# Windowed attention in front of two feed-forward layers: cells of 32 queries by 64 keys, four heads to a unit

## The chip, the cores and the metric

The kernel runs on one core of one Trainium2 chip. The time is device microseconds from launch to end, the median of three runs. TensorE (PE in the profile) multiplies, VectorE (DVE) and ScalarE (ACT) do the elementwise work, SyncE (SP) issues every DMA on one queue. [...]

## The reference

Batch 4, 8 heads, 576 positions, head size 64; 2304 tokens in all, model width 512, hidden width 2048. Everything is fp32.

```python
scores = scale * np.matmul(q, k.transpose(0, 1, 3, 2))
rel = pos[:, None] - pos[None, :]
mask_plain = (rel >= 0) & (rel < 32)                       # heads 0 to 3
mask_dil = (rel >= 0) & (rel < 128) & (rel % 4 == 0)       # heads 4 to 7
attn = softmax of scores where the mask holds, else -1e9
x = np.matmul(attn, v)                                     # (2304, 512)
h = x @ w_in                                               # first layer
g = (a0 + a1*h + a2*h2 + a3*h3) / (1 + |b0|*|h| + |b1|*h2 + 1e-6)
x = g @ w_out
h = x @ w_in2                                              # second layer
out = (max(h, 0) + alpha * min(h, 0)) @ w_out2
```

A query attends to 32 keys at most: the last 32 positions, or, for the dilated heads, 32 positions at a distance of 4. Taken by their remainder modulo 4, the positions of a dilated head form four streams, and in a stream the window is again the last 32.

## The kernel before, in words

The 2304 tokens are six blocks of 384. Attention works in 24 units, U = 0 to 23, four to a block: two plain, then two dilated. Before the change a unit is two heads and two segments of 192 tokens. A plain unit cuts a segment in three tiles of 64 queries by 96 keys, a dilated one in four tiles of 48 by 80. For each unit the code has these steps.

- `att_s` (L444 to L488): the mask is written into PSUM banks aS and aP by bf16 matmuls with an identity (L461), and the scores are added by fp32 matmuls (L481) in 64x64 quarters of the array, four at a time. The profile shows each fp32 matmul of this kind as two MATMUL instructions.
- `att_max` (L495, L499, VectorE), `att_exp` (L515, ScalarE, one instruction for each tile, with a sum), `att_den` (L525, L526), and the normalisation: `att_norm` (L535, ScalarE) or, for units 0 to 3, `att_norm2` (L544, VectorE).
- `att_t` (L552): TensorE transposes each tile into aS and aP. `att_tev` (L571, ScalarE; L573, VectorE, for one of two in units 0 to 3) copies the two banks into the SBUF tile pts.
- `att_pv` (L585): probabilities times values, 128 rows by 64 columns of the array, two at a time, into a bank of the ring ps_h, which has two banks and which the first layer uses too. `att_hi` (L612, ScalarE) copies the result to xh, `att_lo` (L618, VectorE) the rest to xl, since the large matmuls take a value as a high and a low part.

Units 0 to 4 come first. Then a loop over J = 0 to 47 takes two chunks of 128 hidden columns of the first layer at each J: `inproj` (L648) into ps_h, `rat_1` and `rat_2` (L666 to L680) for the rational function, `g_split` (L687, L688), `outproj` of J-2 (L698) into four banks ps_y. For block 0 (J = 0 to 7) the weights are unsplit fp32 (16 MATMUL instructions a J and layer half), later they are split (24 instructions). One unit U = 4 + (J+1)//2 is worked in every two J: at odd J `att_pv(U-1)`, `att_s(U)`, `att_hi(U-1)`, `att_lo(U-1)`, `att_max`, `att_exp`, `att_den`, half of `att_norm`; at even J the other half, `att_t` and `att_tev`. Attention ends with unit 23, before J = 40. `w_convert` (L378 to L399) turns float64 weights into fp32 words on ScalarE and VectorE; `w_early` does so for 13 weight pairs of the second layer from J = 16 on. The second layer (L717, L839 and L745 to L874) has no attention.

A planner, `in_order_of_need`, sets the order of instructions on each engine for the first 197 us from estimated costs (`_cost`); after that program order holds. SyncE's DMAs keep program order; at the start that is the string `ORDER`, in which q and v are the two loads of a unit, w a weight chunk, c the masks, i the fp32 identity, p coefficients.

Of the kernel before, what the change touches and what calls it, by code (L numbers as in the profile page):

```python
# [34 lines left out]
FILL = 256  # L35
ORDERED = 197e3
# [3 lines left out]
ORDER = "cqiqpvqvqvvwwwwwwqvwwwwwwwwqv"  # L40


class Shape:


    def __init__(self, dilated):
        self.dil = dilated
        self.nt = DIL if dilated else 3
        self.nq = SEG // self.nt
        self.nk = self.nq + WIN  # L50
        self.m = 2 * self.nq
        self.rows = 64 + self.nq
        self.step = self.nk if dilated else self.nq
        self.kw = self.nt * self.nk if dilated else SEG + WIN
        self.qk = SEG + self.kw
        self.vw = self.nt * 128
# [46 lines left out]
def _cost(i):  # L103
# [6 lines left out]
    if e == mybir.EngineType.PE:  # L110
        if ins[0].dtype == F32 and not i.is_transpose:
            if n > 128:
                return 645, 845
            return (40, 250) if i.tile_size[0] == 64 else (65, 270)
        if i.is_transpose:
            return 100, 300
        if ins[0].dtype == BF16:
            return (30, 230) if n < 256 else (0.42 * n, 0.42 * n + 200)
        return 0.45 * n, 0.45 * n + 200
# [150 lines left out]
def attn_rational_prelu_kernel(  # L270
    ctx: ExitStack,
    tc: tile.TileContext,
    qk_p: bass.AP,
    v_p: bass.AP,
    qk_d: bass.AP,
    v_d: bass.AP,
# [7 lines left out]
    eye: bass.AP,  # L284
# [26 lines left out]
    ident = cp.tile([128, 128], F32, name="ident")  # L311
    msk = cp.tile([128, consts.shape[1]], BF16, name="msk")
    ident16 = msk[:, 0:128]
    mask = {}
    o = 128
    for dil in (0, 1):
        for first in (0, 1):
            mask[dil, first] = msk[:, o:o + SHAPES[dil].nk]
            o += SHAPES[dil].nk
# [109 lines left out]
    def u_info(U):  # L429
        n, pair = divmod(U, 4)  # L430
        return n, pair, SHAPES[pair // 2]

    def u_load(U, what):
        n, pair, sh = u_info(U)
        i = n * 2 + pair % 2
        if U < 4:
            tag = f"{'in' if what == 'qk' else 'out'}l{8 + 2 * U}"
            t = wp.tile([128, 2 * DM], F32, tag=tag, name="ld_" + what)
        else:
            t = ldp.tile([128, 2 * DM], F32, tag=what, name="ld_" + what)  # L440
        if what == "qk":
            nc.sync.dma_start(out=t[:, :2 * sh.qk], in_=(qk_d if sh.dil else qk_p)[i])
        else:
            nc.sync.dma_start(out=t[:, :2 * sh.vw], in_=(v_d if sh.dil else v_p)[i])  # L444
        att.setdefault(U, {})[what] = t

    QUADS = ((0, 0), (1, 1), (0, 1), (1, 0))

    def att_s(U, tags=("aS", "aP")):

        blk, _, sh = u_info(U)
        a = att[U]
        ld = a["qk"]
        s = a["s"] = [bank(tag) for tag in tags]
        T, n, nq = sh.nt, sh.nk, sh.nq
        base = mask[sh.dil, 0]
        size = (64, nq)

        def put(h, g, t0, t1, mk):
            r = slice(64 * h, 64 * h + 64)  # L460
            nc.tensor.matmul(  # L461
                out=s[h][64 * g:64 * g + size[g], t0 * n:t1 * n].rearrange("p (t k) -> p t k", t=t1 - t0),
                lhsT=ident16[r, 64 * h:64 * h + size[g]],
                rhs=mk[r].unsqueeze(1).to_broadcast([64, t1 - t0, n]),
                start=(t0 == 0), stop=False,
            )

        for h, g in QUADS:
            if (2 * blk + g) % 3:
                put(h, g, 0, T, base)  # L470
            elif sh.dil:
                put(h, g, 0, T, mask[1, 1])
            else:
                put(h, g, 0, 1, mask[0, 1])
                put(h, g, 1, T, base)
        for t in range(T):
            for h, g in QUADS:
                r = slice(64 * h, 64 * h + 64)
                q0 = g * sh.qk + t * nq
                k0 = g * sh.qk + SEG + t * sh.step  # L480
                nc.tensor.matmul(  # L481
                    out=s[h][64 * g:64 * g + size[g], t * n:(t + 1) * n],
                    lhsT=ld[r, q0:q0 + size[g]],
                    rhs=ld[r, k0:k0 + n],
                    start=False, stop=(t == T - 1),
                )

    def att_max(U):  # L488
        _, _, sh = u_info(U)
        a = att[U]  # L490
        T, n, m = sh.nt, sh.nk, sh.rows
        mx = sp.tile([128, 8], F32, tag="mx", name="mx", bufs=2)
        nm = a["nm"] = sp.tile([128, 8], F32, tag="nm", name="nm", bufs=2)
        for h in range(2):
            nc.vector.tensor_reduce(  # L495
                out=mx[:m, h * T:(h + 1) * T], in_=a["s"][h][:m, :T * n].rearrange("p (t k) -> p t k", t=T),
                axis=AX.X, op=ALU.max, negate=True,
            )
        nc.vector.tensor_scalar_mul(out=nm[:m, :2 * T], in0=mx[:m, :2 * T], scalar1=scale)  # L499

    def att_exp(U):
        _, _, sh = u_info(U)
        a = att[U]
        T, n, m = sh.nt, sh.nk, sh.rows
        if U < 4:
            t = tp.tile([128, 2 * BLK], F32, tag="t" + "abca"[U], name="p", bufs=2)
            a["p"] = [t[:, :T * n], t[:, T * n:]]
            a["pp"] = t[:m, :2 * T * n].rearrange("p (t k) -> p t k", k=n)
        else:
            a["p"] = [ap_.tile([128, BLK], F32, tag="p", name="p") for _ in range(2)]  # L510
        sm = a["sm"] = sp.tile([128, 8], F32, tag="sm", name="sm", bufs=2)
        for h in range(2):
            for t in range(T):
                k = h * T + t
                nc.scalar.activation(  # L515
                    out=a["p"][h][:m, t * n:(t + 1) * n], in_=a["s"][h][:m, t * n:(t + 1) * n], func=AF.Exp,
                    scale=scale, bias=a["nm"][:m, k:k + 1], accum_out=sm[:m, k:k + 1],
                )

    def att_den(U):  # L520
        _, _, sh = u_info(U)
        a = att[U]
        w, m = 2 * sh.nt, sh.rows
        rd = a["rd"] = sp.tile([128, 8], F32, tag="rd", name="rd", bufs=2)
        nc.vector.tensor_scalar_add(out=a["sm"][:m, :w], in0=a["sm"][:m, :w], scalar1=1e-9)  # L525
        nc.vector.reciprocal(out=rd[:m, :w], in_=a["sm"][:m, :w])  # L526

    def att_norm(U, h):
        _, _, sh = u_info(U)
        a = att[U]  # L530
        T, n, m = sh.nt, sh.nk, sh.rows
        p, rd = a["p"][h], a["rd"][:, h * T:(h + 1) * T]
        for t in range(T):
            pv = p[:m, t * n:(t + 1) * n]
            nc.scalar.activation(out=pv, in_=pv, func=AF.Copy, scale=rd[:m, t:t + 1])  # L535

    def att_norm2(U):
        _, _, sh = u_info(U)
        a = att[U]
        T, n, m = sh.nt, sh.nk, sh.rows  # L540
        for h in range(2):
            pp = a["pp"][:, h * T:(h + 1) * T]
            rd = a["rd"][:m, h * T:(h + 1) * T].unsqueeze(2).to_broadcast([m, T, n])
            nc.vector.tensor_tensor(out=pp, in0=pp, in1=rd, op=ALU.mult)  # L544

    def att_t(U, h, tag):
        _, _, sh = u_info(U)
        a = att[U]
        T, n, r = sh.nt, sh.nk, sh.rows
        pt = bank(tag)  # L550
        for t in range(T):
# [657 lines left out]
```

## Time and profile before

| | |
|---|---|
| median of three runs | 886.04 us (884.64 to 886.32) |
| profiled execution: span from first to last instruction | 881.9 us |
| PE busy | 870.7 us, 99% |
| DVE busy | 760.0 us, 86% |
| ACT busy | 612.6 us, 69% |
| DMA | 92.78 MB, mean 105 GB/s |

The profiled execution's own time is known as its span; the median of the runs is 4.1 us above that span, for what lies around the first and the last instruction. Busy is the time in which at least one instruction of an engine runs. Matmuls overlap, so the time of one is read from the distance of starts and not from its duration.

### The profile page before, as it was taken

Reading aid. Unit: us, or ns where it says so; the run is one execution under the profiler, and the core shown is the slowest. Engines: PE = TensorE matmul, PEld = TensorE weight load, DVE = VectorE, ACT = ScalarE, POOL = GpSimd, SP = SyncE. Lnnn points to the kernel's source line nnn. Section 1 sums busy time; section 2 is a strip of 40 time slices with the busy share of each in tenths; the row PEclk is TensorE's granted clock in tenths of the full one; section 3 lists DMA queues with packets and bytes.
Section 4 is the critical chain, followed back from the end, with each engine's and each line's share of the span. In section 5 each row is a group of like instructions: output and inputs, shape, how many; then the busy total and the mean of one; then the engine's idle time right before and its main releaser. Section 6 shows DMA issues by size and latency. Waiting matters only on the chain.

```text
span 881.9 us, 14820 instructions
## 1 busy us (share of the span) xinstructions
PE 870.7 (99%) x5744; PEld 778.5 (88%) x5744; DVE 760.0 (86%) x1199; ACT 612.6 (69%) x1253; POOL 0.2 (0%) x4
## 2 busy tenths in 40 slices
PE   8999999999999999999999999999999999999998
PEld 6555679999999999999999999998889989899896
DVE  5999999989899998999999999998986778767652
ACT  6999988787877888887677576557564456645423
POOL 0000000000000000000000000000000000000000
PEclk9999999999999999999999999999999999999999
DMA  9964103124334534443021232323320011210001
GB/s 346 406 259 160 43 25 103 38 91 155 116 123 149 177 119 140 151 132 108 20 78 42 97 130 96 120 84 117 99 85 24 29 44 60 96 48 25 0 1 72
DMA packets 32902, 92.78 MB, mean 105 GB/s; under 512 B 3904, under 2 KB 11328, under 8 KB 32832
## 3 DMA queue, kind: packets, MB, share of 16 engines
q1 hardware_dynamic: 32832, 91.83, 30.1%
q8 instruction: 45, 0.74, 0.4%
q14 instruction: 25, 0.20, 0.1%
HBM read 76.61 MB, written 15.20 MB: 104 GB/s over the span
## 4 chain that ended last, share of the span: by engine, by line
PE 66%; ACT 15%; DVE 14%; DMA 3%; issue 2%; SPq 1%; ACTq 0%; DVEq 0%
PE ps_h L839 19%; PE ps_y L717 14%; PE ps_y L698 12%; PE ps_h L648 11%; PE ps_aS L717 4%; PE ps_aP L717 4%; ACT p L515 3%; ACT p L535 2%; DVE tc L679 2%; DVE tb L678 2%; DVE tc L680 2%; ACT tc L667 2%; ACT ta L676 2%; ACT ta L677 2%; DVE gl L688 1%
## 5 line engine op out<-in xcount | busy, mean ns | idle before, releaser
L648 PE MATMUL ps_h<-xh,winh 128*128 128x384 f32 x320 | 110.2, 344 | 1.9 <-DVE tc L669 1.7
L698 PE MATMUL ps_y<-gh,wouth 128*128 128x384 f32 x320 | 107.9, 339 | 0.0
L698 PE MATMUL ps_y<-gl,wouth 128*128 128x384 f32 x320 | 107.2, 335 | 0.2 <-DVE gl L688 0.2
L698 PE MATMUL ps_y<-gh,woutl 128*128 128x384 f32 x320 | 107.2, 335 | 0.0
L648 PE MATMUL ps_h<-xh,winl 128*128 128x384 f32 x320 | 107.1, 335 | 0.0
L648 PE MATMUL ps_h<-xl,winh 128*128 128x384 f32 x320 | 107.1, 335 | 0.0
L717 PE MATMUL ps_y<-wouth,gl 128*128 128x512 f32 x192 | 74.9, 390 | 0.0
L717 PE MATMUL ps_y<-woutl,gh 128*128 128x512 f32 x192 | 74.9, 390 | 0.0
L717 PE MATMUL ps_y<-wouth,gh 128*128 128x512 f32 x192 | 74.8, 390 | 0.0
L666 ACT ACTIVATE ta<-ps_h,root 128x384 f32<-128x384 f32 x96 | 56.7, 591 | 24.1 <-PE ps_h L648 23.9
L667 ACT ACTIVATE tc<-ps_h,co 128x384 f32<-128x384 f32 x96 | 66.0, 688 | 0.0
L648 PEld LDWEIGHTS ps_h<-xh,winh 128*128 128x128 f32 x320 | 60.0, 188 | 5.9 <-DVE tc L669 3.4
L745 ACT ACTIVATE gh<-tc 128x768 fp32r<-128x768 f32 x48 | 40.4, 841 | 30.5 <-PE ps_aP L717 28.0
L698 PEld LDWEIGHTS ps_y<-gl,wouth 128*128 128x128 f32 x320 | 60.1, 188 | 0.6 <-DVE gl L688 0.5
L648 PEld LDWEIGHTS ps_h<-xl,winh 128*128 128x128 f32 x320 | 60.1, 188 | 0.3
L745 ACT ACTIVATE st_a<-w 128x1024 fp32r<-128x1024 f32 x24 | 25.5, 1061 | 50.1 <-PE ps_h L839 41.5
L746 DVE TENSOR_TENSOR gl<-tc,gh 128x768 fp32r<-128x768 f32 x48 | 45.8, 955 | 16.8 <-ACT gh L745 16.7
L698 PEld LDWEIGHTS ps_y<-gh,wouth 128*128 128x128 f32 x320 | 60.1, 188 | 0.1
L648 PEld LDWEIGHTS ps_h<-xh,winl 128*128 128x128 f32 x320 | 60.1, 188 | 0.0
L698 PEld LDWEIGHTS ps_y<-gh,woutl 128*128 128x128 f32 x320 | 60.0, 188 | 0.0
L678 DVE SCALAR_TENSOR_TENSOR tb<-tb,ta 128x768 f32<-128x768 f32 x48 | 45.7, 953 | 15.4 <-ACT ta L677 15.1
L669 DVE SCALAR_TENSOR_TENSOR tc<-tc,co,ps_h 128x384 f32<-128x384 f32 x96 | 58.3, 608 | 0.5
(197 smaller groups left out, 2313.1 us busy)
## 6 DMA issues: line engine op xcount, KB each, us to landing
w<-w_dram_in SPq DMA_DIRECT2D x24, 512.0 KB, 3.6
raw<-in_w_in_dram SPq DMA_DIRECT2D x16, 512.0 KB, 4.7
raw_inh<-in_w_out_dram SPq DMA_DIRECT2D x13, 512.0 KB, 3.6
ld_qk<-in_qk_d_dram SPq DMA_DIRECT2D x12, 512.0 KB, 5.5
ld_v<-in_v_d_dram SPq DMA_DIRECT2D x12, 512.0 KB, 4.5
ld_qk<-in_qk_p_dram SPq DMA_DIRECT2D x12, 416.0 KB, 4.1
ld_v<-in_v_p_dram SPq DMA_DIRECT2D x12, 384.0 KB, 3.3
y_dram<-os SPq DMA_DIRECT2D x24, 192.0 KB, 1.9
```

Of the source, the lines that this page charges most:

```text
L515: nc.scalar.activation(out=a["p"][h][:m, t * n:(t + 1) * n], in_=a["s"][h][:m, t * n:(t + 1) * n], func=AF.Exp, scale=scale, bias=a["nm"][ ...
L535: nc.scalar.activation(out=pv, in_=pv, func=AF.Copy, scale=rd[:m, t:t + 1])
L648: nc.tensor.matmul(out=hp[:, :BLK], lhsT=w, rhs=x, start=(k == 0), stop=(k == len(pairs) - 1))
L666: nc.scalar.activation(out=ta, in_=hp, func=AF.Abs, scale=root)
L667: nc.scalar.activation(out=tc_, in_=hp, func=AF.Identity, scale=co[:, 3:4], bias=co[:, 2:3])
L669: nc.vector.scalar_tensor_tensor(out=tc_, in0=tc_, scalar=co[:, 1:2], in1=hp, op0=ALU.add, op1=ALU.mult)
L678: nc.vector.scalar_tensor_tensor(out=tb, in0=tb, scalar=C1, in1=ta, op0=ALU.add, op1=ALU.mult)
L698: nc.tensor.matmul(out=yt[:, :BLK], lhsT=w[:, m * 128:(m + 1) * 128], rhs=g, start=(c == 0 and i == 0), stop=(c == NC - 1 and i == len(pai ...
L717: nc.tensor.matmul(out=yt, lhsT=g[:, tok], rhs=w, start=(first and i == 0), stop=(last and i == 2))
L745: nc.scalar.activation(out=hi, in_=t, func=AF.Copy)
L746: nc.vector.tensor_tensor(out=lo, in0=t, in1=hi.bitcast(F32), op=ALU.subtract)
L839: nc.tensor.matmul(out=hp, lhsT=u[:, ws], rhs=x[:, xs], start=(k == 0), stop=(k == 5))
```

## The change

A unit is now four heads (the plain ones or the dilated ones) and 192 queries of each, in six cells of 32 queries by 64 keys; a plain unit is half a block of tokens, a dilated one two of the four streams of a block. Scores are 24 matmuls in 64x32 tiles of the array (eight tiles), the cells alternating between the upper and the lower 64 rows. The mask of a cell is one of four kinds, and neighbouring cells of one kind share a mask matmul. The probabilities of all cells lie in one tile of 128 partitions (32 for each head) by 384 columns. VectorE transposes its 32x32 blocks in one instruction, in place of TensorE's transposes and of their copies out of PSUM. Probabilities times values are matmuls of 32 rows by 64 columns, one for each head and block of 32 keys (28 in a plain unit, 32 in a dilated one), and go into aS and aP instead of ps_h, so `att_hi` and `att_lo` are two instructions of 192 columns each. `att_pv`, `att_hi` and `att_lo` of unit U are moved from the odd J that follows to the even J itself, after `inproj`; `att_s(U)` comes first in the odd J. The fp32 identity and its DMA are gone, queries and values of a unit share a load, and `ORDER` and the planner's costs differ.

```diff
-ORDER = "cqiqpvqvqvvwwwwwwqvwwwwwwwwqv"
+ORDER = "capaaawwwwwwawwwwwwwwa"
...
+        for jj in range(HALF):
+            for i in range(HEADS):
+                for p in range(2):
+                    at = jj * HEADS + i
+                    nc.tensor.matmul(
+                        out=s[p][quad(i), jj * CELL:(jj + 1) * CELL],
+                        lhsT=a["q"][rows(p), at * QB:(at + 1) * QB],
+                        rhs=a["k"][rows(p), at * CELL:(at + 1) * CELL],
+                        start=False, stop=(jj == HALF - 1),
+                    )
...
+        for p in range(2):
+            nc.vector.tensor_reduce(
+                out=mx[:, p * HALF:(p + 1) * HALF], in_=a["s"][p][:, :HALF * CELL].rearrange("p (t k) -> p t k", k=CELL),
+                axis=AX.X, op=ALU.max, negate=True,
             )
...
+        for p in range(2):
+            for jj in range(HALF):
+                j, k = 2 * jj + p, p * HALF + jj
+                nc.scalar.activation(
+                    out=a["p"][:, j * CELL:(j + 1) * CELL], in_=a["s"][p][:, jj * CELL:(jj + 1) * CELL], func=AF.Exp,
+                    scale=scale, bias=a["nm"][:, k:k + 1], accum_out=sm[:, j:j + 1],
...
+    def att_norm(U):
+        a = att[U]
+        for j in range(UB):
+            pv = a["p"][:, j * CELL:(j + 1) * CELL]
+            nc.scalar.activation(out=pv, in_=pv, func=AF.Copy, scale=a["rd"][:, j:j + 1])
...
+        nc.vector.transpose(out=a["r"], in_=a["p"])
...
+        a["ot"] = [bank(tag) for tag in a["tags"]]
+        for g in range(sh.segs):
+            for b in range(-1, sh.nb):
+                c0, c1 = max(b, 0), min(b + 2, sh.nb)
+                v0 = (g * (sh.nb + 1) + b + 1) * D
+                o, r = g * sh.nb * QB, g * sh.nb * CELL
+                for i in range(HEADS):
+                    rows = slice(QB * i, QB * i + QB)
                     nc.tensor.matmul(
+                        out=a["ot"][i // 2][64 * (i % 2):64 * (i % 2) + 64, o + c0 * QB:o + c1 * QB],
+                        lhsT=a["v"][rows, v0:v0 + D],
+                        rhs=a["r"][rows, r + max(b * CELL + QB, 0):r + min((b + 1) * CELL + QB, sh.nb * CELL)],
+                        start=(g == 0 and b == -1), stop=(g == sh.segs - 1 and b == sh.nb - 1),
+                        skip_group_check=True,
                     )
...
+        if new:
+            att_s(U)
         if J % 2 and U <= NU:
-            att_pv(U - 1)
-            if new:
-                att_s(U)
-            att_hi(U - 1)
-            att_lo(U - 1)
-            for what in ("qk", "v"):
-                load_next(what)
+            load_next()
...
         for item in items[2 * J:2 * J + 2]:
             inproj(item)
+        if flip:
+            att_pv(U)
...
         if new:
             att_den(U)
-            att_norm(U, 0)
+            att_norm(U)
         if flip:
-            if J:
-                att_norm(U, 1)
-            for h, tag in enumerate(("aS", "aP")):
-                att_t(U, h, tag)
-                att_tev(U, h)
+            att_hi(U)
+            att_lo(U)
         rat_2(J)
+        if new:
+            att_t(U)
```

## Rows read from the trace of the kernel before

**Rows 1.** The page: busy time of each engine, and the granted clock in slices.
```profile
PE 870.7 (99%) x5744; PEld 778.5 (88%) x5744; DVE 760.0 (86%) x1199; ACT 612.6 (69%) x1253; POOL 0.2 (0%) x4
...
PEclk9999999999999999999999999999999999999999
```
**Rows 2.** Busy time by stretch: start:end, length, busy us (instructions) of each engine, clock, DMA.
```profile
0.00:25.40 25.40, 22.85 (x375) 16.75 (x375) 16.01 (x48) 17.60 (x73) 0.20 (x4) 1.00 0.94 354
25.40:54.00 28.60, 26.42 (x164) 15.57 (x166) 27.70 (x51) 28.52 (x73) 0.00 (x0) 1.00 0.91 360
54.00:202.10 148.10, 148.07 (x1032) 117.52 (x1024) 144.12 (x224) 132.41 (x309) 0.00 (x0) 1.00 0.25 89
202.10:418.50 216.40, 214.51 (x1801) 207.06 (x1800) 198.29 (x320) 176.34 (x454) 0.00 (x0) 1.00 0.42 139
418.50:495.00 76.50, 76.38 (x466) 75.98 (x466) 73.54 (x101) 54.69 (x80) 0.00 (x0) 1.00 0.18 61
```
**Rows 3.** The chain that ended last, two pieces of the start and one after attention.
```profile
13.99 9.95 DMA ld_qk<-in_qk_p_dram
...
26.36 2.00 ACT p L515 x12
...
428.59 4.16 PE ps_h L648 x24
```
**Rows 4.** Timeline of PE over one unit: start, us, instruction, count.
```profile
261.29 1.14 PE L585 MATMUL ps_h<-pts,ld_v 80*64 80x48 f32 x32
262.36 0.31 PE L461 MATMUL ps_aS<-msk 64*64 64x288 bf16 x1
...
263.10 0.44 PE L648 MATMUL ps_h<-xh,winh 128*128 128x384 f32 x1
263.38 0.34 PE L648 MATMUL ps_h<-xl,winh 128*128 128x384 f32 x1
...
275.69 0.49 PE L552 MATMUL ps_aS<-ident,p 128*96 128x128 f32 x3
...
276.27 0.42 PE L698 MATMUL ps_y<-gh,wouth 128*128 128x384 f32 x1
...
280.63 0.92 PE L585 MATMUL ps_h<-pts,ld_v 96*64 96x64 f32 x24
281.48 0.31 PE L461 MATMUL ps_aS<-msk 64*64 64x288 bf16 x1
```
**Rows 5.** Timeline of PE: scores and transposes of a dilated unit.
```profile
242.82 0.32 PE L461 MATMUL ps_aS<-msk 64*64 64x320 bf16 x1
...
242.98 0.23 PE L481 MATMUL ps_aP<-ld_qk 64*48 64x80 f32 x1
...
243.64 0.44 PE L648 MATMUL ps_h<-xh,winh 128*128 128x384 f32 x1
...
256.25 0.55 PE L552 MATMUL ps_aS<-ident,p 112*80 112x112 f32 x4
...
256.95 0.42 PE L698 MATMUL ps_y<-gh,wouth 128*128 128x384 f32 x1
```
**Rows 6.** VectorE and ScalarE, groups by shape: count, busy us, mean ns, idle before.
```profile
L668 DVE TENSOR_TENSOR tc<-tc,ps_h 128x384 f32<-128x384 f32 x96 | 52.6, 548 | 3.9 <-ACT tc L667 3.1
...
L678 DVE SCALAR_TENSOR_TENSOR tb<-tb,ta 128x768 f32<-128x768 f32 x48 | 45.7, 953 | 15.4 <-ACT ta L677 15.1
...
L618 DVE TENSOR_TENSOR xl<-ps_h,xh 128x384 fp32r<-128x384 f32 x20 | 14.1, 706 | 0.4 <-ACT xh L612 0.3
...
L394 DVE SCALAR_TENSOR_TENSOR win<-raw,win 128x512 uint32<-128x512 uint32 x16 | 10.8, 682 | 0.0
...
L571 ACT ACTIVATE pts<-ps_aS 96x384 f32<-96x384 f32 x11 | 5.3, 486 | 0.0
...
L495 DVE TENSOR_REDUCE mx<-ps_aP 128x3 f32<-128x288 f32 x11 | 4.9, 447 | 0.0
...
L495 DVE TENSOR_REDUCE mx<-ps_aP 112x4 f32<-112x320 f32 x10 | 4.8, 478 | 0.0
```
**Rows 7.** Waits between 202 and 420 us: who waited for whom, us, times, longest.
```profile
PE ps_h L648 <- DVE tc L669: 1.7, 4, 0.7
```

More of the change, by code (lines that the diff above doesn't have):

```diff
@@ L47, in __init__, with mask @@
         self.dil = dilated
[L48 to L56, printed above, removed]
+        self.segs = 2 if dilated else 1
+        self.nb = UB // self.segs
+        self.vw = self.segs * (self.nb + 1) * D
+    def mask(self, n, half, j):
+        bb = j % self.nb
+        if self.dil:
+            return {0: 1, 4: 2, 5: 3}.get((3 * n + bb) % 9, 0)
+        return int((12 * n + UB * half + bb) % 18 == 0)
 SHAPES = (Shape(False), Shape(True))
@@ L449, in att_s @@
+        att[U] = {"q": qv[:, :QW], "v": qv[:, QW:QW + sh.vw], "k": kt[:, :KW]}
+    HALF = UB // 2
     def att_s(U, tags=("aS", "aP")):
-        blk, _, sh = u_info(U)
+        n, half_, sh = u_info(U)
         a = att[U]
-        ld = a["qk"]
+        a["tags"] = tags
         s = a["s"] = [bank(tag) for tag in tags]
[L455 to L486, printed above, removed]
+        kinds = [[sh.mask(n, half_, 2 * jj + p) for jj in range(HALF)] for p in range(2)]
@@ new lines, in rows, with quad @@
+        def rows(p):
+            return slice(64 * p, 64 * p + 64)
+        def quad(i):
+            return slice(QB * i, QB * i + QB)
+        runs = [[jj for jj in range(HALF) if jj == 0 or kinds[p][jj] != kinds[p][jj - 1]] for p in range(2)]
+        for step in range(max(map(len, runs))):
+            for i in range(HEADS):
+                for p in range(2):
+                    if step < len(runs[p]):
+                        j0 = runs[p][step]
+                        j1 = (*runs[p], HALF)[step + 1]
+                        nc.tensor.matmul(
+                            out=s[p][quad(i), j0 * CELL:j1 * CELL].rearrange("p (t k) -> p t k", k=CELL),
+                            lhsT=ident16[rows(p), 64 * p:64 * p + QB],
+                            rhs=mask[kinds[p][j0]][rows(p)].unsqueeze(1).to_broadcast([64, j1 - j0, CELL]),
+                            start=(step == 0), stop=False,
+                        )
@@ L537, in att_norm2 @@
     def att_norm2(U):
-        _, _, sh = u_info(U)
         a = att[U]
[L540 to L547, printed above, removed]
-        a = att[U]
-        T, n, r = sh.nt, sh.nk, sh.rows
-        pt = bank(tag)
-        for t in range(T):
-            nc.tensor.transpose(pt[:n, t * r:(t + 1) * r], a["p"][h][:r, t * n:(t + 1) * n], ident[:r, :r])
-        a["pt", h] = pt
@@ L921, in st_pair, with load_next @@
         return rest
-    loads = {what: list(range(NU)) for what in ("qk", "v")}
-    def load_next(what):
-        for U in loads[what][:1]:
-            u_load(loads[what].pop(0), what)
+    loads = list(range(NU))
+    def load_next():
+        if loads:
+            u_load(loads.pop(0))
     def w_pairs(layer):
@@ L1021, in attn_rational_prelu_kernel @@
     att_den(4)
-    for h in range(2):
-        att_norm(4, h)
+    att_norm(4)
+    att_t(4)
     for J in range(NP):
@@ L1173, in _pack_attention @@
+        arrays += [qv, kk]
     return arrays
```

239 lines of the change are left out of this document (99 added, 140 removed).

## The prediction

> **What bounds the kernel.** The page comes first: PE is busy 99% of the span at the full clock, DVE 86%, ACT 69% [rows 1]. One average hides several stages, so the second view is the busy time by stretch [rows 2]. After 418.5 us there is no attention, and the change can only shift that part. From 202.1 to 418.5 us PE is busy 214.5 of 216.4 us and DVE 198.3 (92%). From 54 to 202.1 us PE has no gap and DVE is busy 144.1 of 148.1 (97%). From 25.4 to 54 us ACT is full (28.5 of 28.6), and the first 25.4 us are loads: the DMA engines are 94% busy, and the chain sits on one load until 23.94 us [rows 2, 3]. So the reader should see PE as the bound from 54 us on, and DVE close behind it.
>
> The third view is the timeline of PE over one unit, that is two J [rows 4]. The two J's large matmuls are 96 starts; 24 take 4.16 us [rows 3], so 16.64 us. The unit shown takes 280.63 - 261.29 = 19.34 us, so attention costs PE 2.70 us. Its terms: values 1.07 (dilated) and 0.85 (plain, 281.48 - 280.63); scores with masks 0.74 (plain) [rows 4] and 0.82 (dilated) [rows 5]; transposes 0.58 and 0.70 [rows 4, 5]. The first large matmul behind small ones starts its successor after 0.28 instead of 0.17: 0.11 for each way back. Between 276.27 and 280.63, 24 matmuls take 4.36: 0.11 for the way back and 0.09 for the way in [rows 4]. A plain unit costs 0.09 + 0.85 + 0.74 + 0.11 + 0.58 + 0.11 = 2.48, a dilated one 2.90, the mean 2.69. Eleven units of 16.64 + 2.69 make 212.6 of the 216.4 us between 202.1 and 418.5; the other 3.8 are waits, such as 1.7 us for DVE to free ps_h [rows 7].
>
> **TensorE's part.** The transposes go: 0.58 and 0.70. Scores: before, 32 instructions of 80 columns take 0.66 us, the way out included [rows 5], in eight steps of four, 0.083 a step. The new unit has 48 instructions of 64 columns; if eight tiles run at once these are six steps of 0.083 x 64/80 = 0.066, together 0.40. Masks lead in for 0.16 [rows 5], and I keep that: there are 9 (plain) and 17 (dilated) on the mean, but shorter ones. Scores come to 0.56. The other bound is that small matmuls don't start closer on the mean than now, 0.66/32 = 0.0206: then 57 or 65 instructions take 1.18 or 1.34. I take 0.56, because rows 5 show four starts inside one step, which is what streaming, not issue, would give.
>
> [...]
>
> Values: the new instructions are 56 (plain) and 64 (dilated), four at a time in four groups of rows: 14 and 16 steps. The steps of two took 0.85/12 = 0.071 and 1.07/16 = 0.067 [rows 4] whether 64 or 48 columns ran, so I take 0.98 and 1.07. Bounds: 0.0206 for each instruction (1.15 and 1.32), and half the step where 32 columns run (0.85).
>
> Values and scores no longer stand together, so each has its own 0.09 in and 0.11 out. Plain: 0.09 + 0.56 + 0.11 + 0.09 + 0.98 + 0.11 = 1.94, dilated 2.03: 0.54 and 0.87 less, mean 0.70. Behind 25.4 us some 19.5 units count (20 of values, 19 of scores): 13.7 us of PE.
>
> **VectorE's part.** This decides how much of that is seen. The transpose of 384 columns shows in no row. Nearest is an instruction of the same size, 0.55 [rows 6]; above lies 0.95, if it needs two passes (768 columns), below 0.34 (half of the faster 512-column form, 0.68, is 0.34). I take 0.55. [...] Maxima: 0.45 for 288 and 0.48 for 320 columns [rows 6], so about 0.36 for 192; the two save 0.18 or 0.24. `att_lo` in two halves pays its fixed part twice: from 0.55 at 384 and 0.95 at 768 columns that part is 0.145. Sum of a steady unit: 0.55 - 0.21 + 0.145 = +0.48. Units 0 to 3 lose an eviction of 0.55 and about 0.37 of `att_norm2` each.
>
> **ScalarE's part.** Two evictions of 0.49 go [rows 6]; a dilated unit has two exponentials and two normalisations fewer, and `att_hi` pays a second start: some 1.2 us less in a plain unit, 2 in a dilated one. Past 54 us ACT has room, so this counts only at the start.
>
> **Sum by stretch.** To 54 us: ACT, full there, does units 4 and 5 with about 3 us less and units 0 to 3 without their evictions (2 us); the loads for four units shrink by 0.3 MB, under 1 us at 354 GB/s [rows 2], but the score load of unit 4 still ends near 23.9 us. I take 3 us, bounds 1 and 5. From 54 to 202.1 us: seven units take 4.9 us off PE, to 143.2, and put 3.4 on DVE, to 147.5; DVE becomes the bound. Gain 1 us, bounds -1 and 5. From 202.1 to 418.5 us: PE needs 212.6 - 7.7 = 204.9, DVE 198.3 + 5.3 = 203.6. They nearly meet. Before, 3.8 us of waits stood on top with DVE at 92%; I allow 5, so 210, gain 6.5, bounds 2 and 11.5. Together 10.5: the span falls from 881.9 to about 871.4, and with the 4.1 us around it from 886 to 875.5; I say 876.
>
> The moved steps: with `att_pv` inside the even J, `att_s` of the next odd J waits until `att_lo` has emptied aS and aP. Behind that wait stand all of the J's large matmuls. From the end of `inproj` to that point PE has values and 24 matmuls, 5.1 us; ACT and DVE need about 3.1 for two `rat_1` chains and the halves of hi and lo (0.55 to 0.71 for each operation of 384 columns [rows 6]). So 2 us hide it when DVE is not behind. In return ps_h has one user fewer, which takes away the waits of rows 7. The second load of a unit needs the values of the unit before last to be done, which now happens earlier; y and weight DMAs queue behind it on SP as before.
>
> **Rivals.**
> - *TensorE's whole gain is seen*, because DVE fills its gaps: 13.7 + 3.8 + 3 = 20 us, 866. For: ACT is relieved and hands DVE its work sooner. Against: DVE's 97% between 54 and 202 us.
> - *VectorE takes it back*: a transpose costs 0.95. DVE then needs 150.3 us in the second stretch, a loss of 2, and 208 in the third, where with 5 of waits 3 are left; with 1 from the start, 884.
> - *Small matmuls don't pack by eight* (the slower side, and the case in which the change doesn't do what it says). At 0.0206 for each, a plain unit costs PE 0.4 + 1.18 + 1.15 = 2.73, a dilated one 3.06: 0.2 worse, 4 us in 19.5 units, and DVE's +0.48 another 2 in waits; with 1 back from the start, 891. It decides from a mean distance of the score and mask instructions of 20.5 ns: 61 x 0.0205 = 1.25 is 0.56 + 0.70. [...]
> - *The new wait on `att_lo`*: a converted weight pair puts 0.68 x 5 = 3.4 us on DVE at once [rows 6], 1.4 more than the slack of 2; half of that in each of 13 J is 9 us, and the gain shrinks to 1: 885.
>
> **Chances.** Forecast 0.47 (870 to 881 by itself), whole gain 0.16, VectorE 0.12, packing 0.14, new wait 0.11. A run of this kernel tells 0.2% (1.8 us) from no change. Faster: 0.47 + 0.16 and half or less of the two that end near no change, 0.73; same 0.10; slower 0.17. The range is 866 to 887: it takes in all but the packing case and part of the others.
>
> **What would show it.** Right: scores of a unit take PE near 0.56 us, values near 1.0, L552 and L571 are gone, DVE's transpose reads about 550 ns, DVE is 96% or more busy from 202 us to the end of attention, that end comes near 408 us, and the second layer is unchanged. Wrong: more than 1.2 us for the scores; a transpose near 0.95; PE idle in front of the score or mask matmuls with `att_lo` or `att_hi` as releaser; or PE idle that grows as fast as its work shrinks.

## The result, and the profile after

The changed kernel takes 889.56 us (median of 5 runs, 887.76 to 892.1), the kernel before beside it 884.64. The ratio is 1.0056, interval 1.0038 to 1.0073: slower by 0.6%, where 876 was forecast. The profiled span is 887.6 us, 5.7 more than before.

The page after: the lines that answer to [rows 1], and from its DMA part the queue that carries instructions (packets, MB, share).

```profile
PE 862.5 (97%) x7031; PEld 765.5 (86%) x7032; DVE 761.9 (86%) x1235; ACT 579.5 (65%) x1165; POOL 0.2 (0%) x4
...
PEclk9899999999999999999999999999999999999999
...
q8 instruction: 55, 0.90, 0.4%
```

PE has more instructions and is less busy; the clock row is no longer all 9. In the lines of the kernel after, L472 are the masks, L482 the scores, L553 the values, L618 and L668 the large matmuls of the first layer, L539 is VectorE's transpose, L526 ScalarE's normalisation, L646 Ln and L647 Exp. Busy time by stretch, which answers to [rows 2] (start:end, length, PE, PEld, DVE, ACT, POOL, clock, DMA share, GB/s):

```profile
0.00:25.40 25.40, 18.32 (x499) 13.02 (x500) 11.43 (x40) 11.33 (x58) 0.20 (x4) 0.99 0.92 343
25.40:54.00 28.60, 25.70 (x301) 15.04 (x294) 24.58 (x49) 23.95 (x69) 0.00 (x0) 0.89 0.82 314
54.00:202.10 148.10, 143.38 (x1406) 109.96 (x1405) 143.55 (x237) 120.25 (x272) 0.00 (x0) 1.00 0.26 91
202.10:418.50 216.40, 210.45 (x2390) 200.35 (x2389) 201.94 (x344) 162.81 (x415) 0.00 (x0) 1.00 0.40 135
418.50:495.00 76.50, 76.50 (x500) 76.21 (x500) 74.93 (x103) 52.95 (x80) 0.00 (x0) 1.00 0.13 42
```

Up to 54 us ACT is 11 us less busy than in [rows 2] and no longer full. From 54 to 202 us PE has 4.7 us without work where it had none, from 202 to 418 us 5.9 instead of 1.9. PE's work shrank, and idle time came in its place.

Where the time went is read from the first `rat_1` instruction on ScalarE (L666 before, L636 after) of chosen J, in the two traces, in us:

| | J=0 | J=3 | J=17 | J=17 to 41 | end |
|---|---|---|---|---|---|
| before | 28.2 | 58.7 | 207.0 | 232.0 | 881.9 |
| after | 33.4 | 62.8 | 212.1 | 232.3 | 887.6 |

In these two profiles 4.2 us are lost by J = 3, 1.0 up to J = 17, 0.2 from there to J = 41 and 0.3 behind. The forecast by the same stretches was -3, -1, -6.5 and 0. A single profile places such a loss only roughly. Five profiles with the start of the kernel after (this one and four of the runs below) have J = 3 between 61.5 and 62.9 and J = 17 between 211.3 and 212.6; the two with the start of the kernel before have 58.7 and 61.7, and 207.0 and 210.0. At J = 17 all five are later than the two, by 1.3 to 5.6 us. From J = 3 to J = 17 alone the five take 149.3 to 150.1 us, the two 148.3 both, so 1 to 1.8 us are lost there. Two questions follow: what delays the start, and where the steady part's gain went.

**The start.** PE in the start of the kernel after: start, us, instruction, count, and in brackets the idle time ahead.

```profile
16.12 0.44 PE L482 MATMUL ps_y<-ld_out,ld_in 64*32 64x64 f32 x29
18.61 0.41 PE L482 MATMUL ps_y<-ld_out,ld_in 64*32 64x64 f32 x19 [2.05 <-issue]
...
21.88 0.86 PE L553 MATMUL ps_y<-p,ld_in 32*64 32x32 f32 x39 [0.27 <-DVE p L539]
24.74 0.54 PE L553 MATMUL ps_y<-p,ld_in 32*64 32x32 f32 x12 [2.01 <-issue]
```

Twice PE stops for 2 us in the middle of one unit's scores or values, and waits for nothing that the profile shows. Both stops lie on the chain that ended last:

```profile
16.57 2.05 issue
...
22.73 2.01 issue
```

Then the clock falls (start:end, length, PE busy, clock, DMA share, GB/s):

```profile
16.00:18.00 2.00, 0.57 (x31) 1.00 1.04 412
...
22.00:24.00 2.00, 0.73 (x39) 1.00 1.03 402
24.00:26.00 2.00, 1.26 (x41) 0.72 1.02 402
26.00:28.00 2.00, 2.00 (x65) 0.50 1.04 414
28.00:30.00 2.00, 2.00 (x4) 0.50 1.02 397
30.00:32.00 2.00, 2.00 (x29) 0.58 1.03 412
```

Behind the two pieces of idle time PE is granted half clock, 0.50 from 24.86 to 31.69 us, 6.8 us in all; block 0's first large matmuls begin in it, at 27.7 us. In the kernel before, the same stretch has clock 1.00 [rows 2], and PE has no wait under the name issue up to 54 us (its weight loads have one of 1.0).

**The steady part.** One plain unit's scores after, from the first mask to the large matmuls behind them; it answers to [rows 4, 5]:

```profile
285.93 0.20 PE L472 MATMUL ps_aS<-msk 64*32 64x64 bf16 x1
...
286.06 0.21 PE L482 MATMUL ps_aS<-ld_v,ld_qk 64*32 64x64 f32 x1
...
286.56 0.22 PE L482 MATMUL ps_aP<-ld_v,ld_qk 64*32 64x64 f32 x1
286.71 0.44 PE L618 MATMUL ps_h<-xh,winh 128*128 128x384 f32 x1
```

0.13 us of masks and 0.65 of scores. A record is one MATMUL of the trace. With the way out to the first large matmul the 48 score records take 0.65/48 = 13.5 ns each. Their starts alone are 10.6 ns apart on the mean, about 7 among the first eight and 13 at the end. They spread over 0.50 us, with 0.15 of way out behind them. In the kernel before the last score of the unit in rows 5 is

```profile
243.48 0.23 PE L481 MATMUL ps_aP<-ld_qk 64*64 64x80 f32 x1
```

so its 0.66 us are 0.50 between the first start and the last, in steps of 0.07, and 0.16 of way out. Undisturbed, the block of masks and scores after takes 0.72 to 0.81 in all units from J = 17 on; the values take 0.95 (plain) and 1.06 (dilated).

The waits of 0.2 us and more from 211 to 443 us, J = 17 to 41 (engine, waiting instruction, releaser: us, times, longest); PE's answer to [rows 7]:

```profile
PE ps_h L618 <- DVE tc L639: 3.9, 6, 0.9
PE ps_aS L553 <- DVE pts L539: 1.1, 2, 0.9
PE ps_aP L472 <- DVE xl L588: 0.6, 2, 0.4
...
DVE tb L648 <- ACT ta L647: 5.7, 10, 1.8
DVE pts L539 <- ACT p L526: 4.0, 4, 1.6
```

In the same J of the kernel before, PE's waits come to 1.5 + 0.2 = 1.7 us:

```profile
PE ps_h L648 <- DVE tc L669: 1.5, 3, 0.7
...
PE ps_y L698 <- DVE gl L688: 0.2, 1, 0.2
```

Here they come to 5.8, with a last one of 0.2. Seven profiles with the steady code of the kernel after have 3.7 to 5.8 us of such waits (mean 4.9), two with that of the kernel before 1.7 and 2.0. Without the waits the 24 J take 225.3 to 226.9 us in the seven and 230.3 and 231.3 in the two: TensorE's own part shrank by some 4.5 us, and its waits grew by some 3. One odd J on ScalarE and VectorE shows the order behind them:

```profile
296.37 1.55 ACT L526 ACTIVATE p<-p,rd 128x64 f32<-128x64 f32 x6 [1.08 <-DVE rd L520]
297.82 0.92 ACT L646 ACTIVATE ta<-tb,c1t 128x768 f32<-128x768 f32 x1
...
297.95 0.58 DVE L539 STREAM_TRANSPOSE pts<-p 128x384 f32<-128x384 f32 x1 [0.78 <-ACT p L526]
300.30 0.96 DVE L648 SCALAR_TENSOR_TENSOR tb<-tb,ta 128x768 f32<-128x768 f32 x1 [1.77 <-ACT ta L647]
```

All six normalisations now stand in the odd J ahead of Ln (L646). Before, half of them did. VectorE had finished L645 at 297.17, Ln starts 0.65 us later behind the normalisation, and VectorE waits 0.78 for the normalisation and 1.77 for Exp.

### The profile page after: what moved, and what is told of

It is laid out like the page before. It is cut to its first block, busy times and chain, and to the rows that moved or that the text cites. A ratio compares the mean times of both kernels' runs of the same rounds, so it can differ in the third digit from the quotient of the medians.

```text
span 887.6 us, 17356 instructions
## 1 busy us (share of the span) xinstructions
PE 862.5 (97%) x7031; PEld 765.5 (86%) x7032; DVE 761.9 (86%) x1235; ACT 579.5 (65%) x1165; POOL 0.2 (0%) x4
## 4 chain that ended last, share of the span: by engine, by line
PE 61%; DVE 19%; ACT 13%; DMA 4%; issue 2%; SPq 0%; ACTq 0%
PE ps_h L809 19%; PE ps_y L687 14%; PE ps_h L618 9%; PE ps_y L668 9%; PE ps_aS L687 4%; PE ps_aP L687 4%; DVE tc L649 2%; DVE tb L648 2%; ACT p L511 2%; DVE tb L645 2%; ACT tc L637 2%; DVE tc L650 2%; ACT p L526 2%; DVE tc L638 2%; DVE tc L639 2%
## 5 line engine op out<-in xcount | busy, mean ns | idle before, releaser
L618 PE MATMUL ps_h<-xh,winh 128*128 128x384 f32 x320 | 110.2, 344 | 6.8 <-DVE tc L639 6.8
L668 PE MATMUL ps_y<-gh,wouth 128*128 128x384 f32 x320 | 108.0, 338 | 0.0
L668 PE MATMUL ps_y<-gl,wouth 128*128 128x384 f32 x320 | 107.3, 335 | 0.0
L668 PE MATMUL ps_y<-gh,woutl 128*128 128x384 f32 x320 | 107.2, 335 | 0.0
L618 PE MATMUL ps_h<-xh,winl 128*128 128x384 f32 x320 | 107.1, 335 | 0.0
L618 PE MATMUL ps_h<-xl,winh 128*128 128x384 f32 x320 | 107.0, 334 | 0.0
L636 ACT ACTIVATE ta<-ps_h,root 128x384 f32<-128x384 f32 x96 | 56.2, 586 | 26.9 <-PE ps_h L618 22.8
L618 PEld LDWEIGHTS ps_h<-xh,winh 128*128 128x128 f32 x320 | 60.0, 188 | 12.1 <-DVE tc L639 10.5
L657 ACT ACTIVATE gh<-tc 128x768 fp32r<-128x768 f32 x40 | 34.1, 851 | 44.2 <-DVE tc L650 44.1
L668 PEld LDWEIGHTS ps_y<-gh,wouth 128*128 128x128 f32 x320 | 60.0, 188 | 0.4
L715 ACT ACTIVATE gh<-tc 128x768 fp32r<-128x768 f32 x48 | 40.4, 841 | 30.5 <-PE ps_aP L687 28.0
L618 PEld LDWEIGHTS ps_h<-xl,winh 128*128 128x128 f32 x320 | 60.1, 188 | 0.1
L668 PEld LDWEIGHTS ps_y<-gl,wouth 128*128 128x128 f32 x320 | 60.1, 188 | 0.1
L668 PEld LDWEIGHTS ps_y<-gh,woutl 128*128 128x128 f32 x320 | 60.1, 188 | 0.1
L618 PEld LDWEIGHTS ps_h<-xh,winl 128*128 128x128 f32 x320 | 60.1, 188 | 0.0
```

The source lines that it names most:

```text
L618: nc.tensor.matmul(out=hp[:, :BLK], lhsT=w, rhs=x, start=(k == 0), stop=(k == len(pairs) - 1))
L636: nc.scalar.activation(out=ta, in_=hp, func=AF.Abs, scale=root)
L657: nc.scalar.activation(out=hi, in_=g, func=AF.Copy)
L668: nc.tensor.matmul(out=yt[:, :BLK], lhsT=w[:, m * 128:(m + 1) * 128], rhs=g, start=(c == 0 and i == 0), stop=(c == NC - 1 and i == len(pai ...
L715: nc.scalar.activation(out=hi, in_=t, func=AF.Copy)
```

## The experiments

All medians stand beside runs of the kernel before on the same chip; ratios are to it, after is 1.0056. "Steady" is the time from J = 17 to J = 41 in the profile. Seven profiles that have the steady code of the kernel after gave 230.1 to 232.5 (mean 231.2), two that have that of the kernel before 232.0 and 233.3. So a steady time of one profile is good to about 1 us, and the change gained some 1.5 us there.

### Which engine sets the steady part

First run: no VectorE transpose in units 13 to 23.

```
         a = att[U]
+        if U >= 13:
+            a["r"] = a["p"]
+            return
```

> The kernel after, without the VectorE transpose in units 13 to 23 (all behind 202 us); their values then read the untransposed probabilities, so the output is not the reference's. That takes 11 x 0.575 = 6.3 us off VectorE and nothing off TensorE. Theory H (behind 202 us the chain of VectorE and ScalarE that hands ps_h back sets the period): 4 to 7 us faster than the kernel after, about 884. Theory P (TensorE's own instruction time sets it, and the small matmuls cost more than forecast): within 1 us of 889.6.

Measured: 888.59, 1.0053 (1.0035 to 1.0072); steady 231.8. Theory H falls: 6.3 us of VectorE are gone and nothing is seen. VectorE's largest wait in those J:

```profile
DVE tb L651 <- ACT ta L650: 13.1, 12, 2.3
```

It was 5.7 + 4.0 with the transpose. The transpose had filled time in which VectorE waits for ScalarE anyway.

Second run: a third of the scores in units 13 to 23.

```
-        for jj in range(HALF):
+        for jj in range(HALF - 1 if U >= 13 else 0, HALF):
```

> The kernel after with only the last 16 of the 48 fp32 score instructions in units 13 to 23 (the masks are still written; the output is not the reference's). That takes some 11 x 0.42 = 4.6 us off TensorE and nothing off VectorE or ScalarE. Theory H: 0 to 1.5 us faster than 889.6, and TensorE's idle time grows by the rest. Theory P: 4 to 5 us faster, about 885.

Measured: 883.38, 0.9983 (0.9971 to 0.9996); steady 225.3. Theory P, and more than it asked: 6.2 us by the medians. Where nothing disturbs it, the block of masks and scores, 0.72 to 0.81 us before this edit, takes 0.31 or 0.32 in most units and 0.45 to 0.50 in three. A fall by 0.45 for 32 records is 14 ns each. Over 11 units that is 4 to 5 us, and all of PE's waits of 0.2 us and more fall from 5.8 to 2.9.

Third run: a third of the TensorE transposes in the kernel before, units 13 to 23.

```
-        for t in range(T):
+        for t in range(1 if U >= 13 else T):
             nc.tensor.transpose(...)
...
```

> The kernel before with only the first tile of each bank transposed on TensorE in units 13 to 23; the evictions read that tile three or four times, so ScalarE and VectorE do as much as before (the output is not the reference's). That takes about 0.38 (plain) and 0.5 (dilated), together some 4.8 us, off TensorE. Theory P, the bound that was forecast for the kernel before: 4 to 5 us faster than 884.6. Theory H: 0 to 1.5 us faster.

Measured: 880.59, 0.9955 (0.9938 to 0.9972), 3.9 us below the kernel before; steady 228.1 for 232.0. TensorE was the bound in the kernel before too, and four fifths of the 4.8 us that were to be taken off it are seen.

Fourth run: the normalisation behind Ln and Exp.

```
         nc.scalar.activation(out=ta, in_=ta, func=AF.Exp, scale=-1.0)
+        if U is not None:
+            att_norm(U)
...
-            att_norm(U)
```

> The kernel after with the six normalisations of ScalarE moved behind Ln and Exp of the same J instead of ahead of them, nothing else. In the trace after, Ln stood 0.65 us behind them and VectorE then waited 1.8 us for Exp and 0.8 us for the normalisation in one J. Theory H: those waits shrink and the kernel is 1 to 5 us faster, 884.5 to 888.5. Theory P: within 1 us of 889.6.

Measured: 886.96, 1.0027 (1.0016 to 1.0037); steady 229.1. It takes no instruction away. The wait of VectorE's transpose for the normalisation is gone, and PE waits 1.3 us for ps_h instead of 3.9:

```profile
PE ps_y L670 <- DVE gl L660: 1.6, 1, 1.6
PE ps_h L618 <- DVE tc L639: 1.3, 4, 0.5
```

But a wait for VectorE's part of `g_split`, 1.6 us, is new, so PE's waits fall from 5.8 to 3.6 in all. Five profiles with this edit and the tiled masks gave 229.1 to 229.8, below all seven without it; with whole-array masks (below) two gave 229.7 and 231.0. So theory P holds for the length of PE's own work, and the order on ScalarE costs something on top: 2.6 us by the medians here, 1.3 with the old start (below). How is not shown: over the five profiles PE's waits are 4.3 us on the mean, only 0.6 less than over the seven.

Fifth run: both, the normalisation behind and no transposes (diffs as above).

> The kernel after with the normalisation behind Ln and Exp, as in the run before, and without the VectorE transposes of units 13 to 23 (the output is not the reference's). If the transposes cost nothing earlier only because VectorE had to wait for ScalarE in that place, they count now: 3 to 6 us faster than the 887.0 of that run, about 882. If VectorE's work does not set the period at all: within 1 us of 887.0.

Measured: 887.93, 1.0036 (1.0019 to 1.0053); steady 229.8. VectorE's work does not set the period, with the waits for ScalarE mended or not.

Sixth run: each mask by one matmul of the whole array.

```
-            for i in range(HEADS):
...
-                            lhsT=ident16[rows(p), 64 * p:64 * p + QB],
...
+                        lhsT=ident16,
+                        rhs=mask[kinds[p][j0]].unsqueeze(1).to_broadcast([128, j1 - j0, CELL]),
```

> The kernel after with each mask written by one matmul of the whole array in place of four 64x32 tiles: 2 to 5 records a unit for 8 to 20, the same PSUM contents. Theory F for the start: some 35 records fewer, 1.7 us of supply. TensorE as the bound behind 202 us: some 10 records a unit less at about 14 ns, less the wider instruction, 0 to 1.5 us in 11 units. Together 1 to 3 us faster, 886.5 to 888.5. If neither holds: within 1 us of 889.6.

Measured: 885.99, 1.0028 (1.0016 to 1.0039); steady 231.0. The medians fall by 3.6 us, a little more than was asked, but not for the reason given: there are fewer records, but the block of masks and scores takes 0.93 us where nothing disturbs it, 0.2 more than with tiles, and J = 0 comes no earlier (34.2). The profile is of the slowest of the nine executions (888.53), so it can't show where the 3.6 us come from; that is open.

### What delays the start

More small records in units 0 to 3 of the kernel before:

```
-        for t in range(T):
+        for t in [*range(T - 1 if U < 4 else 0), *range(T - 1 if U < 4 else 0), *range(T)]:
```

> The kernel before with the scores of all tiles but the last taken three times in units 0 to 3 (160 more small TensorE records of the start, about as many as the change adds there; the output is not the reference's). Their work is some 3 us on an engine that has fills to give up in that time. Theory F: idle pieces of about 2 us labelled issue appear in the start, and the kernel is 2 to 6 us slower than 884.6. If only the work counts: no such piece, at most 1.5 us slower.

Measured: 891.41, 1.0077 (1.0059 to 1.0095), 7.3 us slower. The kernel before, which had no such piece, now has one under issue, and then a lower clock:

```profile
20.27 0.28 PE L461 MATMUL ps_aP<-msk 64*64 64x288 bf16 x1 [2.60 <-issue]
```

```profile
18.00:22.00 4.00, 1.73 (x14) 0.95 1.00 397
22.00:26.00 4.00, 4.00 (x26) 0.62 1.03 402
```

PE stops at the same places of the start in several kernels, counted in its matmul records: after 347 and 474 of them in the kernel after (2.05 and 2.01 us) and in the one with fewer fills below (1.63 and 3.78), after 220 and 347 in the one with a third of the scores in units 0 to 3 below (2.45 and 1.34). These are 127 apart, and the instruction queue of the kernel after brings 0.90 MB in 55 packets, 16 KB each. The packets' own times in the traces, beside PE's records (us):

| kernel | record | begins | next packet begins, ends | the record 127 later begins | idle before it |
|---|---|---|---|---|---|
| before | 221 | 16.94 | 20.92, 22.03 | 24.38 | 0 |
| after | 221 | 12.50 | 16.26, 17.33 | 18.61 | 2.0 |
| after | 348 | 18.61 | 22.31, 23.41 | 24.74 | 2.0 |
| fewer fills (below) | 348 | 18.50 | 22.25, 23.50 | 24.95 | 3.8 |
| no weight loads (below) | 348 | 23.44 | 24.39, 25.49 | 29.16 | 0 |
| no weight loads (below) | 475 | 29.16 | 30.00, 30.95 | 32.06 | 0 |

In the kernel after a packet starts some 3.7 us after PE has entered the 127 records before its own, takes 1.1, and PE goes on 1.3 later: 6.1 us for 127 records, 48 ns each. In the table PE stands still where it had used them up before the packet had landed. 127 matmul records with their weight loads are 254 instructions. Over the whole span the kernel after has 7031 and 7032 of the two kinds for its 55 packets, and the kernel before 5744 of each for 45: 127.8 and 127.6 of each to a packet.

Next run: no weight loads in the start.

```
         t = wp.tile(...)
+        if key[0] == 1 and n_raw[1] <= 14:
+            nc.gpsimd.memset(t, 0)
+            raw_t[key] = t
+            return
         nc.sync.dma_start(out=t, ...)
```

> The kernel after with the first 14 weight chunks of the start (7.3 MB) written as zeros by GpSimd instead of loaded, so that the DMA engines are not full between 12 and 38 us (the output is not the reference's). Theory F1 (instructions come late because their DMA shares the engines with the loads): the two idle pieces labelled issue go or fall below 0.5 us, the granted clock stays at 1.00 behind 24 us, and 3 to 6 us come back, about 885. Theory F2 (the fetch is as slow without other traffic; it is only the rate of small instructions): both pieces of 2 us stay.

Measured: 880.21, 0.9953 (0.9932 to 0.9975). The windows where the DMA engines are empty:

```profile
22.00:26.00 4.00, 3.14 (x95) 0.95 0.06 22
26.00:30.00 4.00, 2.98 (x146) 1.00 0.03 8
```

There a packet starts 0.95 and 0.84 us after the 127 records before its own are entered, not 3.7, and 127 records then run in 2.9 us without a stop (table): theory F1, the loads delay it. The run doesn't show more: the first `rat_1` of J = 0 comes at 35.2, later than after. With zeros in place of loads VectorE takes the weight conversions ahead of a unit's maxima, PE waits 5.1 us for these, and the clock is 0.70 from 14 to 18 us and 0.50 from 18 to 22. What is gained comes behind J = 3: from there to J = 17 this kernel is 6.1 us shorter than after, and why is open.

The loads of the start with q and k ahead of v:

```
-ORDER = "capaaawwwwwwawwwwwwwwa"
+ORDER = "cqpqvqvqvvwwwwwwqvwwwwwwwwqv"
...
```

> The kernel after with the start's loads in the order of the kernel before: q and k of a unit first, v later, for units 0 to 5. Theory L (the start is late because v now rides ahead of the next unit's scores): the scores of unit 1 begin near 7 us instead of 10.3, and 2 to 4 us of the 5 lost at the start come back, about 886.5. Theory F (TensorE stands still when 128 of its instructions are used up before the next 16 KB of instructions have come, at 16.6 and 22.7 us): both idle pieces of 2 us labelled issue stay, and with them most of the loss; within 1.5 us of 889.6.

Measured: 888.93, 1.0048 (1.003 to 1.0065); one idle piece of 2.7 us under issue stays, and two of 0.5. Theory L falls.

The weight chunks of block 0 ahead of the next unit's loads:

```
-        if J % 2 and U <= NU:
+        if J % 2 and U <= NU and J >= NC // 2:
             load_next()
...
             w_loads(1, 4)
+            if J % 2:
+                load_next()
```

> The kernel after with load_next moved behind w_loads in the J of block 0, nothing else. In the trace after, the load of q and v of unit 6 waited 6.6 us on SP for the values of unit 4 (they end at 42.3 us), and the weight chunks for the next J stood behind it; before, the same chunks went out from 36.4 us on without a wait. Theory W (this hold is what makes J = 3 and the J behind it late): the first rat_1 of J = 3 comes 2 to 4 us earlier and stays so, 886 to 887.5. Otherwise: within 1 us of 889.6.

Measured: 888.37, 1.0046 (1.003 to 1.0061), J = 3 at 63.1. The hold of 6.6 us on SP is real, but it isn't what makes J = 3 late; the 1.2 us of the medians lie inside the two intervals. Theory W falls.

Fewer and longer fills (matmuls of the mask tile in the start whose result nobody reads; they occupy TensorE where it would stand idle):

```
-FILLS = (64,)
+FILLS = (34,)
...
-FILL = 256
+FILL = 480
...
```

> The kernel after with 34 fills of 480 columns in place of 64 of 256: the same work of TensorE in 30 instructions fewer at the start. Theory F (in the start TensorE can't have more than 128 matmul records in some 6.1 us): 30 records fewer are 1.4 us of supply, the idle pieces labelled issue shrink or move by that much, 0.5 to 1.5 us faster, 888 to 889. If the stalls don't set the start: 889.6 within 1.

Measured: 885.71, 1.0015 (1.0005 to 1.0025). That is 3.9 us by the medians, more than was asked, but not where it was asked: J = 0 and J = 3 are 0.5 us earlier (32.9, 62.3), inside the scatter of single profiles, and PE, with less to do, reaches record 474 sooner and stands there longer:

```profile
24.95 0.34 PE L472 MATMUL ps_aP<-msk 64*32 64x192 bf16 x1 [3.78 <-issue]
```

Its stops come to 5.4 us, more than the 4.1 of the kernel after. The profile has 2.2 us of the gain between J = 17 and J = 41, whose code is the same, and 1.1 behind; where the 3.9 come from is open.

A third of the scores in units 0 to 3 (the diff of the second run, with `U < 4`):

> The kernel after with only the last 16 of the 48 score records in units 0 to 3 (128 records of the start fewer; the output is not the reference's). Their work is 4 x 0.4 = 1.7 us of an engine that has 5 us to spare there. Theory F (no more than 128 matmul records in some 6.2 us reach TensorE while the DMA engines are full): the idle pieces labelled issue go or shrink below 1 us, the granted clock stays at 1.00 or falls less, the first rat_1 of J = 0 and of J = 3 comes 3 to 5 us earlier, about 885.5. If the late start has another cause: at most 1 us faster.

Measured: 888.18, 1.0046 (1.0028 to 1.0064); J = 0 at 31.8, J = 3 at 61.2. That is a third of what theory F asked, and neither the medians nor the two times differ from the kernel after by more than the noise. The idle pieces are still there, at records 220 (2.5 us) and 347 (1.3): PE came to record 220 at 14.8 us and went on at 17.56; the packet for the records behind began 5.4 us after the 127 before them were entered. Taking these records away moved the stops and did not end them.

Units 0 to 3 as in the kernel before, all others as after, the run that tells whether the loss lies in these units (the other steps are exchanged in the same way):

```
+            (old_att_s if k < 4 else att_s)(k, sets[(k + 2) % 3])
...
+            (old_att_max if k < 4 else att_max)(k)
+            (old_att_exp if k < 4 else att_exp)(k)
...
```

> The kernel after for the units from 4 on, with units 0 to 3 computed as in the kernel before (its loads, masks, 64x64 tiles and TensorE transposes). If the whole loss lies in the start (theory F, some 220 matmul records more ahead of J = 0 than can be supplied), 4 to 5 us come back and the new cells are as fast as the old ones from then on: 884.5 to 885.5, the same as the kernel before. If the new cells also lose later: 886.5 or more.

Measured: 885.07, 1.0008 (0.9999 to 1.0018): 4.5 us back. The first two stretches:

```profile
0.00:25.40 25.40, 23.34 (x352) 16.99 (x352) 15.17 (x46) 17.42 (x74) 0.20 (x4) 1.00 0.93 345
25.40:54.00 28.60, 25.27 (x282) 14.43 (x283) 26.82 (x53) 26.26 (x71) 0.00 (x0) 1.00 0.92 364
```

No idle piece under issue, clock 1.00, J = 3 at 58.8 as before, and PE takes 6.8 and 6.9 us for 127 records ahead of record 348, just more than the supply's 6.1. Two things stay open. The run puts back the old loads, tiles, TensorE transposes and evictions at once, so it names the units and not which of these steps. And from J = 3 to J = 17 it takes 150.6 us, as slow as after, for 148.3 before: that loss is not one of the start. It is made up from J = 17 to 41, in 230.7 us for 232.0 and 233.3, and by some 0.5 behind.

### Together

> The run before with the normalisation of ScalarE behind Ln and Exp of the same J. If the two losses lie in separate places and add: 881.5 to 883, below the kernel before by 0.2 to 0.35%. If the second hides behind the first: 884 to 885.5.

Measured: 883.81, 0.9991 (0.998 to 1.0002). The two losses add in part, 1.3 us below the run before; the kernel is at best 0.2% faster than before. Three combinations on the start of the kernel after:

> The kernel after with three edits at once: weights ahead of load_next in block 0, 34 long fills for 64, and the normalisation behind Ln and Exp. If the three losses are separate places and add: 889.6 - 3 - 1 - 2.6 = 883, 1 to 2 us below the kernel before. If they hide behind one another: 886 to 887.

> The three edits of the run before and the loads of the start with q and k ahead of v. The order of the loads alone was worth 0.6 us: 882.5 if it adds, the same as the run before if not.

> Weights ahead of load_next in block 0, long fills, normalisation behind Ln and Exp (885.0 together), and the whole-array masks. If the masks' records count at the start and in the steady part: 882.5 to 884, below the kernel before. If the places hide behind one another: 885.

Measured: 885.04 (1.0008, 0.9997 to 1.002), 885.06 (1.0000, 0.9988 to 1.0011) and 887.19 (1.0043, 1.0029 to 1.0057). The gains do not add, and the late start stays (J = 3 at 62.0, 63.0, 64.5). With the whole-array masks the third is 2.2 us slower than the first, though alone they gave 3.6; why is open.

> As the run before, with 12 long fills in place of 34: 22 records fewer, 1.1 us of supply, against more idle time of TensorE between 6 and 20 us, behind which the granted clock may fall to half. Theory F: 0.5 to 1 us faster than the run before, if the clock stays up there; 1 to 3 us slower if it falls.

Measured: 886.69, 1.0021 (1.0009 to 1.0033): 0.5 us below the run before it, inside the two intervals, and J = 3 2.7 us earlier (61.8). The clock was 0.50 from 14 to 30 us and 0.89 from 30 to 34, and the loss of 1 to 3 us that was expected for that case did not come.

## Why the prediction was wrong

- *"To 54 us ... I take 3 us."* This step failed, by some 7 us in the two profiles. It priced the start by ScalarE's relief alone. The relief came, but TensorE had 571 records ahead of J = 0 where it had 374, the DMA engines were full, and it could not get them in time: two stops of 2 us on the chain that ended last, half clock behind them, then ScalarE and VectorE without work. The old start gives back 4.5 us by the medians. That the supply limits PE is shown by the places of the stops, by the packets' times and by the run that made stops in the kernel before. That the stops make all of the 4.5 is not shown: runs that took records away only moved them, and the kernel with fewer fills has more of them and is 3.9 us faster.
- *TensorE's part, scores 0.56.* Mis-sized. Eight tiles pack only in part: starts come at 7 ns at first, but 48 records take 0.65 and not 0.40; with masks 0.72 to 0.81. The starts of the 48 spread over as long a time as those of the 32 before, 0.50 us, where six steps of 0.07 x 64/80 would spread over 0.28. Values (0.98 and 1.07 forecast, 0.95 and 1.06 measured) and the transposes taken away were right. The saving of a unit is so about 0.70 - 0.2 = 0.5, in 11 units some 5.5 us and not 7.7; without waits the profiles show some 4.5.
- *"From 202.1 to 418.5 us ... I allow 5."* This failed too, by some 5 us: the gain is about 1.5 (231.2 on the mean of the seven profiles, for 232.0 and 233.3), not 6.5. PE was the bound, as forecast, before and after. But PE's waits of 0.2 us and more grew from 1.7 and 2.0 to 4.9 on the mean, where the forecast let its waits grow by 1.2 only, from 3.8 to 5. A moved step that the prediction did not price has a part in it: the second half of `att_norm`, from the even J to the odd one, ahead of Ln. Moved behind, 2.6 us come back by the medians. Why the waits grew, that step aside, stays open.
- *From 54 to 202.1 us, gain 1.* It lost 1 to 1.8 us between J = 3 and J = 17 in the five profiles, and 2.2 with the old start: at the end of the bounds and beyond it. VectorE is 97% busy as before, and PE's saving became 4.7 us of idle time, as was argued.
- *VectorE's part.* The sizes were right: the transpose 0.575 (0.55 forecast), the maxima 0.35 (0.36), lo 0.43 a half. Their weight was not: 6.3 us less of VectorE's work changed nothing behind 202 us.
- *The rivals.* "Packing" named the right sign and nearly the right time (891) by luck, with the wrong mechanism: the distance of scores and masks together is 11 to 13 ns, way out included, not above 20.5. The new wait on `att_lo` is 0.8 us in 24 J. "VectorE takes it back" is excluded by the transpose's 0.575 and by the run without it.
- *What would show it.* Values, L552 and L571 gone, the transpose and an unchanged second layer came true; scores, VectorE above 96% (93%) and attention's end (about 5 us later, not 10 earlier) did not. Of the signs of being wrong, PE idle that grows as its work shrinks came, by some 3 us for 4.5.

## What to carry to other kernels

Where large instructions become many small ones, count instructions as well as busy time: divide each stretch's TensorE records by the rate at which they can be supplied there (here one in 48 ns), above all in a start in which the loads fill the DMA engines. When one engine's work shrinks, list for each step that moved which instruction it now stands ahead of on its new engine and who waits for that; a gain on the bound is lost again if the waits grow as fast (here some 3 of 4.5 us). And take work away from each engine in turn before believing a busy share: here 6.3 us taken off a VectorE that is 93% busy changed nothing, and 4 to 5 us taken off a TensorE that is 97% busy gave 6.2. And a single profile places a loss of a few us only roughly: the same start differed by up to 3 us from one profile to the next.

## What the runs showed of the hardware

- Instructions reach TensorE in packets of 16 KB, in the start one for 127 matmul records with their weight loads. With the DMA engines full (share 0.9 and more) a packet began 3.3 to 4.0 us after the 127 records before its own were entered in the starts of the kernels before and after, 5.4 in the run with a third of the scores in units 0 to 3; with them nearly empty (0.06 and 0.03, no weight loads) it was 0.95 and 0.84. A packet took 0.9 to 1.25, and a TensorE that stood still went on 1.3 to 1.45 later. The profile calls the gap issue.
- In the unit at 286 us of the kernel after, matmul records on tiles of 64x32 start 7 ns apart at first and 10.6 ns on the mean, 13.5 with the way out to the next large matmul; with a third of the scores, 32 records fewer saved 14 ns each in most units.
- Masks written by the whole array just ahead of tiled matmuls (the run with whole-array masks) made the block 0.93 us, 0.2 longer than masks in the tiles (0.72).
- Behind two stops of 2 us the granted clock was 0.50 for 6.8 us in the kernel after. A lower clock also came without such a stop: in the run with a third of the TensorE transposes, which has the start of the kernel before, it was 0.94 on the mean from 25.4 to 54 us, and none of PE's waits there stands under issue.
